# Layernorm roots taken for two tiles at once, and a new instruction order: a two-layer attention and MLP kernel

## The chip, the cores and the metric

One core of a Trainium2 chip. The metric is the device time of one execution in microseconds (us); most executions of one kernel agree within 0.3%. TensorE does the matmuls, VectorE (DVE in the profile) and ScalarE (ACT) the elementwise work, GpSimd (POOL) a little of it, and SyncE (SP) issues transfers.

## The reference

Two layers over x of 2048 rows and 512 columns, 32 heads of 16. Each has a linear attention with softmax features and a gated MLP, both behind a layernorm:

```python
def _A_ref(x, wqkv, w_phi, wo):
    q, k, v = ...                                  # x @ wqkv, 32 heads of 16
    pq, pk = q @ w_phi, k @ w_phi                  # per head
    phi_q = concat([softmax(pq), softmax(-pq)]); phi_k = the same of pk
    kv, z = phi_k^T v, sum(phi_k)                  # sums over all 2048 rows
    return (phi_q @ kv / (phi_q @ z + 1e-6)) @ wo
def _B_ref(x, W_gate, W_up, W_down):
    return (relu(x @ W_gate) * (x @ W_up)) @ W_down
for layer in range(2):                             # same weights twice
    x = x + _A_ref(layernorm(x), ...); x = x + _B_ref(layernorm(x), ...)
```

The sum over all rows in `kv` matters here: no attention of a layer can start before the keys of all 16 tiles of 128 rows are done. So a layer has a key stage, a seam, and then attention and MLP tiles; keys of layer 1 run beside the MLP of layer 0.

## The kernel before

The kernel describes each piece of work as an `op` with an engine, a planned cost in ns and a priority (`DUE`), and lets a small planner simulate the engines and write the program in the planned order. `DUE` (2117 numbers) and `PLACE` (301 bits, which of two engines takes an eviction or a scaling) were found by a search over planned time. The normalisation in front of the keys is this:

```python
ACT1 = (190, 297)                    # planned ns: how long the engine is taken, when the result is there
ACT0 = (95, 205)
SUMS = (8 * 40, 8 * 40 + 170)        # the eight key-sum matmuls of a tile ("kvz")
...
def norm_A(l, t, due, after, how):
    _, mv, rs, ln = st[l, "A"]
    a = stats(l, "A", t, due, after)                      # VectorE: bn_stats, bn_aggr
    a = op("ACT", ACT1, due, lambda: nc.scalar.activation(
        out=ln[:, t:t + 1], in_=mv[:, t, 1:2], func=AF.Ln, scale=1.0, bias=eps[:]), [a, c_eps], name="ln")
    a = op("ACT", ACT0, due, lambda: nc.scalar.activation(
        out=rs[:, t:t + 1], in_=ln[:, t:t + 1], func=AF.Exp, scale=-0.5), [a], name="rstd")
    xn = Buf(p_xn)
    n = op("DVE", SCALE, due, lambda: nc.vector.tensor_scalar(...), [a], [xn], name="xnA", port=True)
    ...                                                   # then turned by a transfer or by TensorE
```

1 / sqrt(variance + eps) is exp(-0.5 ln(variance + eps)), on one column per tile: 128 rows, one number each. The planner itself, cut:

```python
def plan(ops):
    ...
    for e, cand in open_.items():       # of every engine: what could start first; DUE decides among equals
        ...
        o = min((o for t, o in at if t <= first + 1), key=rank)
    ...
    clock[o.eng] = t + occ              # engines run their instructions strictly in this order
```

The softmax here doesn't subtract the row's maximum and nothing guards it: scores larger than these inputs give would overflow.

Of the kernel before, what the change touches and what calls it, by code (L numbers as in the profile page):

```python
# [8 lines left out]
P = 128  # L9
D = 512  # L10
H = 32
# [196 lines left out]
SUMS = (8 * 40, 8 * 40 + 170)  # L208
# [12 lines left out]
class K:  # L221
# [9 lines left out]
    "0000010100000000000000000000000001000000000001000000010000010000111000100010000011100010000000001100"  # L231
    "1110100001101000000001001111110001111111000111101111011101100100001001010011001101100101101011001010"
    "0111100111000000000111000001000000011010011000110100110100010010010010011111011011010111101111110001"
    "1"
)
PHI = dict(POOL=("POOL", "POOL"), DVE=("DVE", "DVE"), BOTH=("DVE", "POOL"))
PHI0 = ["POOL", "POOL", "DVE"] * 5 + ["BOTH"]
BLOCKS = ((1, 1, 2, 4, 4, 2, 2), (1, 1, 2, 4, 4, 2, 1, 1))
# [4 lines left out]
    171312045, 171176422, 171176382, 171108352, 171198950, 171077496, 171191852, 171044825, 171078679, 171078698,  # L243
    171075562, 172890511, 176979114, 171233483, 169157194, 169158347, 169158293, 172028606, 169159557, 172030067,
    175144900, 173911508, 175144538, 171845769, 169157815, 171893840, 172460034, 171325700, 171787868, 171042634,
    171000808, 171921057, 170984535, 171039910, 171020854, 171061543, 170544187, 171018809, 171804656, 171138113,
    171042055, 171921054, 166325450, 171843476, 171894266, 172913174, 172651099, 171841824, 172662070, 171803244,
    170856605, 171671995, 171013294, 171049523, 171011469, 170882211, 170861860, 170773832, 171088096, 171173941,
    166032751, 171021263, 171024027, 165980719, 171010636, 170972794, 170819202, 170901748, 170120315, 170882262,
    171029170, 171058781, 171028664, 170882214, 170773339, 170644736, 171176421, 170834144, 170500271, 171024600,  # L250
    171023816, 171671545, 170881567, 170973450, 170924320, 170862256, 171733328, 171027555, 171028689, 170104438,
    170987569, 171023551, 171017586, 170995073, 171010979, 171010010, 167097015, 171025767, 171021114, 170976230,
    171009963, 170940900, 170707416, 170903149, 170861679, 170895382, 170987736, 170805774, 171134539, 171029304,
    171015238, 170840189, 171086712, 170868324, 172856244, 171023850, 170972541, 170882265, 170862137, 170938874,
    171078382, 171074459, 171076295, 170781572, 171024964, 171027552, 170806858, 171027495, 171045955, 171031024,
    170994249, 171063885, 171044941, 170994211, 171021566, 171025728, 170861672, 170773342, 171004053, 171050973,
    171041308, 166032748, 171017859, 170995571, 172857251, 170995217, 171021462, 171036003, 171036000, 171021133,
    171034376, 171019328, 171026473, 170901529, 171024967, 170970509, 170994580, 171076245, 171039727, 174124623,
    167096153, 170995703, 170993965, 172856241, 171391510, 169375356, 166303781, 170203837, 171046298, 171045973,
    171020654, 171025772, 171029618, 171031289, 171018943, 171009668, 171040302, 212653769, 170870934, 170529933,  # L260
    171034876, 170993625, 171023605, 170674343, 170471544, 170946591, 173676712, 171046899, 170942347, 170973537,
    170992325, 171016031, 171004733, 170995129, 171046905, 171039117, 171046765, 170882142, 171036586, 171036549,
    170994607, 171035366, 171017772, 171035774, 166304101, 171351583, 171019187, 170346706, 170971352, 171020568,
    171004375, 171003406, 171019334, 170304741, 171357616, 166452149, 166304120, 171079347, 166362383, 171167760,
    171117024, 166253921, 166338723, 171040796, 171047078, 171026685, 169377831, 171021245, 170994356, 170993118,
    36276708, 36035224, 170174038, 170250060, 171018957, 171021288, 171052769, 171039826, 171052600, 171024073,
    170912232, 170912229, 171041278, 171041091, 171026709, 170998266, 170996907, 171023919, 171166970, 170791395,
    170174888, 36033968, 171014267, 166253845, 171052882, 170955784, 170370511, 171069861, 171052009, 171114979,
    171018524, 171021870, 166290380, 169376343, 170080981, 170529851, 171023791, 170744874, 36538735, 169932483,
    167242939, 166340952, 169222540, 171015285, 166253698, 171075807, 171049021, 171048078, 171040769, 171046830,  # L270
    170951770, 171034112, 171019616, 162145965, 166306292, 168062450, 170989765, 170738642, 171014079, 171052180,
    171053152, 171029348, 171107467, 171116988, 171052395, 171052101, 171047241, 171018507, 166291021, 170394652,
    170241606, 169841292, 169839339, 171025410, 36538707, 169011552, 170955744, 171035785, 170982203, 171011859,
    172910993, 171019677, 171107459, 171053563, 171019442, 170965939, 171116604, 170396198, 170371650, 170946958,
    170908940, 171025481, 169342071, 170739641, 170936868, 171053246, 171052141, 170955698, 171107296, 170969038,
    171023612, 171023814, 171022273, 170966052, 166242691, 170739300, 170739634, 172357143, 171546744, 169010552,
    36035209, 171416052, 171078698, 171044839, 171075311, 170998783, 171032340, 170924317, 170900084, 170081843,
    171086886, 170990356, 171026585, 173042630, 173042922, 173042517, 168321289, 172879342, 173042568, 168321051,
    172927323, 170992379, 172910634, 171038768, 170968444, 171030324, 171014479, 173212841, 171391944, 166303271,
    170994206, 171041364, 171020312, 171051951, 171058190, 170965859, 171041907, 169841329, 171055174, 171052230,  # L280
    170942705, 170942434, 171085553, 171076047, 171053056, 171145237, 171076497, 171074528, 171014605, 171056526,
    171051703, 171087793, 171055202, 171055199, 173107373, 171046402, 171075427, 171142525, 171076401, 171076133,
    171040387, 171077324, 171053025, 173106718, 171076475, 171076472, 171151969, 171055262, 171076461, 165027616,
    171071476, 171071476, 171021261, 171071470, 166364733, 170933205, 171071456, 171072557, 166583114, 166634328,
    170763740, 171064949, 171064956, 167452684, 171029994, 171034997, 171028062, 174965392, 171024521, 171067273,
    171075410, 171025877, 171066819, 171039121, 171025885, 171074446, 171043144, 171024040, 178726974, 174950080,
    178814041, 171074432, 170065497, 171030810, 167260056, 171030866, 170939768, 171027739, 172713143, 170846670,
    171027934, 171030090, 171029521, 171029163, 171042670, 170921361, 172866657, 170417020, 170585755, 170756076,
    169426177, 167510585, 170739334, 171054335, 170496052, 171026814, 171033593, 171037765, 171030610, 170922766,
    170611363, 171028464, 171030272, 168112842, 166271274, 166270840, 166270101, 169191803, 170915073, 171067239,  # L290
    169457441, 171028842, 168543918, 171030184, 170611592, 171035872, 171030051, 170924132, 170923368, 171030620,
    170915873, 170906849, 171068641, 170774900, 174317953, 170772708, 172787245, 174802385, 171548595, 177175587,
    170194011, 171030804, 171031467, 171031553, 171031404, 169172838, 169173200, 171030929, 171031335, 171031355,
    168543946, 162962369, 162963842, 170874511, 171383560, 170476373, 171046401, 171033853, 170289040, 171030586,
    168965534, 170924236, 171030926, 171037386, 171031635, 171030844, 170775025, 170870650, 170774436, 170503270,
    170503425, 168543850, 170673934, 170673801, 171546738, 171032639, 170471129, 171030697, 171031009, 171031310,
    171031944, 170801875, 171025213, 171031797, 171025213, 171024587, 170509377, 170340672, 170301702, 170301316,
# [161 lines left out]
def kernel(  # L459
# [194 lines left out]
    def norm_A(l, t, due, after, how):  # L654
# [9 lines left out]
            op1=Alu.mult), [a], [xn], name="xnA", port=True)  # L664
        c, i = t // C, t % C
        return turn(xn, lambda: xnTA[c][:, :, i * P:(i + 1) * P], how, due, n, [], [], "xnTA",
                    XPOSE if l else XPOSE_LOADS)


    class Keys:  # L670
# [346 lines left out]
```

## Time and profile before

| | before |
|---|---|
| time, us | 387.9 median of 6 (387.68 to 388.77) |
| span of the profiled run, us | 386.3 |
| busy, us: TensorE / VectorE / ScalarE / GpSimd | 374.1 / 315.3 / 212.0 / 45.3 |
| matmul and weight-load records | 2787 and 2831 |

Busy TensorE is recorded with overlapping matmuls, and 44 matmul records are missing from this trace, so it can't be compared between kernels. I use **TensorE's lost time** instead: I go through the weight loads, whose records are complete, give each the spacing that its matmul has where matmuls run back to back (0.216 us for 512 columns down to 0.0325 for 65), and note when each sum of work is reached. The time that passes less the work that is done is what TensorE lost. All of the program's work is about 367 us.

### The profile page before, as it was taken

How to read it: one execution, taken by the hardware profiler on the slowest of the kernel's cores; microseconds unless marked ns; L12 is line 12 of the kernel's file. 1: busy time of each engine (PE TensorE's matmuls, PEld its weight loads, DVE VectorE, ACT ScalarE, POOL GpSimd, SP SyncE). 2: the span in 40 equal slices, each digit the busy share in tenths (PEclk: the TensorE clock that was granted, in tenths of full speed). 3: DMA queues.
4: the chain of work that ended last, by engine and by line, in shares of the span. 5: the costliest groups of instructions: out<-in, count | busy, mean ns of one | idle time of the engine just before them, and what ended most of it. 6: DMA issues, size and time to landing. Idle time of an engine off the chain costs nothing.

```text
span 386.3 us, 7626 instructions
## 1 busy us (share of the span) xinstructions
PE 374.1 (97%) x2787; PEld 225.2 (58%) x2831; DVE 315.3 (82%) x799; ACT 212.0 (55%) x559; POOL 45.3 (12%) x46
## 2 busy tenths in 40 slices
PE   8989998999999999999999999999999999999996
PEld 4544454877654445445766755587865445447585
DVE  7999999999999889838875776899998999544244
ACT  5989988654456314554555669975435411422131
POOL 0433810000021000202222224000000000000000
PEclk9999999999999999999999999999999999999999
DMA  8469740232323224301101100013322234001020
GB/s 228 124 159 240 173 120 1 33 60 56 75 35 63 30 41 65 60 15 26 24 14 22 27 3 1 2 31 61 76 62 63 30 69 97 14 14 49 14 63 29
DMA packets 60869, 22.83 MB, mean 59 GB/s; under 512 B 52672, under 2 KB 59808, under 8 KB 60832
## 3 DMA queue, kind: packets, MB, share of 16 engines
q1 hardware_dynamic: 60416, 21.95, 26.2%
q8 instruction: 22, 0.36, 0.4%
q10 hardware_dynamic: 416, 0.39, 0.3%
q14 instruction: 15, 0.12, 0.1%
HBM read 7.91 MB, written 2.10 MB: 26 GB/s over the span
## 4 chain that ended last, share of the span: by engine, by line
PE 76%; DVE 9%; ACT 3%; issue 2%; DMA 2%; POOL 0%; DVEq 0%; ACTq 0%
PE b L874 34%; PE b L907 19%; PE b L810 6%; PE b L682 4%; PE b L688 4%; PE q L778 3%; PE b L850 2%; ACT Eq L764 2%; PE b L760 2%; DVE sk L693 2%; PE q L719 1%; DVE phiK L702 1%; DMA oT<-o 1%; DVE bstA L651 1%; DMA xnTA<-xn 1%
## 5 line engine op out<-in xcount | busy, mean ns | idle before, releaser
L874 PE MATMUL b<-xnTB,wgu 128*128 128x128 bf16 (+2 forms) x1192 | 150.1, 279 | 0.7 <-ACT xnTB L604 0.3
L874 PEld LDWEIGHTS <-wgu 128*128 128x128 bf16 x1200 | 97.3, 98 | 42.7 <-issue 0.4
L878 ACT ACTIVATE gu<-b 128x512 bf16<-128x512 f32 (+1 forms) x83 | 48.1, 584 | 67.0 <-PE b L874 63.0
L907 PE MATMUL b<-wd,hT 128*128 128x512 bf16 (+2 forms) x348 | 81.8, 372 | 0.8
L702 POOL TENSOR_TENSOR phiK<-ek,sk 128x512 bf16<-128x512 bf16 x40 | 44.6, 1133 | 191.3 <-ACT sk L698 106.1
L907 PEld LDWEIGHTS <-hT 128*128 128x128 bf16 (+1 forms) x363 | 34.5, 98 | 35.0 <-DVE hT L882 0.3
L882 DVE TENSOR_TENSOR hT<-gu 128x512 bf16<-128x512 bf16 (+1 forms) x83 | 33.5, 408 | 16.5 <-ACT gu L604 14.9
L685 ACT ACTIVATE ek<-b 128x512 bf16<-128x512 f32 x64 | 36.6, 626 | 14.1 <-PE b L682 14.0
L693 DVE TENSOR_REDUCE sk<-ek 128x64 f32<-128x1024 bf16 x32 | 38.6, 1208 | 6.8 <-ACT ek L685 5.8
L605 DVE CAST gu<-b 128x512 bf16<-128x512 f32 (+1 forms) x42 | 28.0, 669 | 15.7 <-PE b L874 15.7
L764 ACT ACTIVATE Eq<-b 128x512 bf16<-128x512 f32 x64 | 36.1, 631 | 1.7 <-PE b L760 0.9
L604 ACT CAST gu<-b 128x512 bf16<-128x512 f32 (+1 forms) x41 | 23.2, 565 | 22.8 <-PE b L874 21.8
L682 PE MATMUL b<-Wk,xnTA 128*128 128x512 bf16 x122 | 32.1, 379 | 1.6 <-DMA xnTA<-xn 1.2
L810 PE MATMUL b<-wo,oT 128*128 128x512 bf16 x125 | 32.4, 379 | 0.7 <-DMA oT<-o 0.4
L688 PE MATMUL b<-wv,xnTA 128*128 128x512 bf16 x120 | 31.9, 379 | 1.0 <-ACT xnTA L604 0.3
L760 PE MATMUL b<-xnTA,Wq 128*128 128x512 bf16 x125 | 30.9, 379 | 0.2
L914 DVE SCALAR_TENSOR_TENSOR X<-b,rsB,X 128x512 bf16<-128x512 f32 (+1 forms) x33 | 23.8, 730 | 7.5 <-PE b L907 7.2
L778 PE MATMUL q<-R,Eq 128*128 128x144 bf16 x256 | 27.8, 226 | 1.4 <-ACT DS L604 0.8
L604 ACT CAST N<-q 128x384 bf16<-128x384 f32 (+1 forms) x60 | 26.7, 466 | 4.1 <-DVE pr L803 2.9
L778 PEld LDWEIGHTS <-Eq 128*128 128x128 bf16 x256 | 20.3, 98 | 11.8 <-issue 2.2
L814 DVE TENSOR_TENSOR X<-X,b 128x512 bf16<-128x512 bf16 x32 | 21.4, 675 | 5.0 <-PE b L810 4.7
L855 ACT ACTIVATE gr<-b 128x192 bf16<-128x192 f32 (+1 forms) x19 | 5.8, 308 | 31.8 <-PE b L850 31.8
(70 smaller groups left out, 408.9 us busy)
## 6 DMA issues: line engine op xcount, KB each, us to landing
out_dram<-X SPq DMA_DIRECT2D x15, 128.0 KB, 1.8
X<-in_A_x_dram SPq DMA_DIRECT2D x6, 256.0 KB, 3.4
wgu<-in_B_W_gate_dram SPq DMA_DIRECT2D x4, 344.0 KB, 3.7
wgu<-in_B_W_up_dram SPq DMA_DIRECT2D x4, 344.0 KB, 3.6
wd<-in_B_W_down_dram SPq DMA_DIRECT2D x5, 256.0 KB, 4.9
wv<-in_A_wqkv_dram SPq DMA_DIRECT2D x2, 256.0 KB, 4.3
wo<-in_A_wo_dram SPq DMA_DIRECT2D x4, 128.0 KB, 3.4
oT<-o SPq DMA_TRANSPOSE x28, 2.4
```

The costliest lines, as they stand in the source:

```text
L604: both = {"ACT": ("ACT", act(cols), lambda: nc.scalar.copy(out=out_(), in_=in_()), False), "DVE": ("DVE", dve(cols), lambda: nc.vector.ten ...
L682: k = op("PE", mm(4, 512), due, lambda: [nc.tensor.matmul(kp.t[:], lhsT=xnTA[c][:, b, cols], rhs=Wk2[:, b, :], start=(b == 0), stop=(b == ...
L688: v = op("PE", mm(4, 512), due_v, lambda: [nc.tensor.matmul(vp.t[:], lhsT=xnTA[c][:, b, cols], rhs=wv[:, b, :], start=(b == 0), stop=(b == ...
L693: a = op("DVE", SUM16, due, lambda: nc.vector.tensor_reduce(out=sk.t[:], in_=ek.t[:].rearrange("p g s (h f) -> p (g s h) f", f=DH), axis=A ...
L702: e.tensor_tensor(out=ph.t[:].rearrange("p g s (h f) -> p (g s h) f", f=DH)[:, lo:lo + n], in0=ek.t[:].rearrange("p g s (h f) -> p (g s h) ...
L760: q = op("PE", mm(4, 512), due(c, b), lambda b=b, qp=qp: [nc.tensor.matmul(qp.t[:], lhsT=Wq2[:, m, b * P:(b + 1) * P], rhs=xnTA[c][:, m, : ...
L764: done.append(op("ACT", act(512), due(c, b), lambda b=b, s=s, qp=qp: nc.scalar.activation(out=Eq[c][:, b, s, :], in_=qp.t[:], func=AF.Exp, ...
L778: pe.append(op("PE", mm(len(groups), GE), due, lambda ps=ps, groups=groups: [nc.tensor.matmul(ps.t[:, n * GE:(n + 1) * GE], lhsT=Eq[c][:, ...
L810: a = op("PE", mm(4, 512), due + 3, lambda: [nc.tensor.matmul(yp.t[:], lhsT=oT.t[:, b, :], rhs=wo[:, b, :], start=(b == 0), stop=(b == NB ...
L874: nc.tensor.matmul(ps.t[:, q * W:(q + 1) * W], lhsT=wgu[:, s, b, g * P:(g + 1) * P], rhs=xT.t[:, b, 0:W], start=(b == 0), stop=(b == NB - 1))
L878: nc.scalar.activation(out=gu.t[:, 0, 0:cols], in_=gp.t[:, 0:cols], func=AF.Relu)
L907: nc.tensor.matmul(yp.t[:, 0:c1 - c0], lhsT=h.t[:m, f * W + i * P:f * W + (i + 1) * P], rhs=wd[:m, f, c0:c1], start=(f == 0), stop=(f == N ...
```

## The change

Its intent: fewer of the small ScalarE instructions in the first stage, where ScalarE is full; a truer planned cost of the key sums; and an order found by a new search that also varies when the engines start. The core of the diff (the tables of 2117 and 2105 priorities and the placement bits are cut):

```diff
-SUMS = (8 * 40, 8 * 40 + 170)
+RLN, REXP = ((150, 265), (203, 318)), ((145, 262), (198, 315))
+SUMS = (8 * 32.5, 8 * 32.5 + 170)
 PLACE = (  ... 109 of 301 bits differ ...
+PAIRN, PAIRK = 4, T
 DUE = (    ... every number differs ...
-    def norm_A(l, t, due, after, how):
+    def norm_A(l, tiles, dues, afters, hows):
-        a = stats(l, "A", t, due, after)
+        t0, n = tiles[0], len(tiles)
+        seen = [stats(l, "A", t, due, after) for t, due, after in zip(tiles, dues, afters)]
-            out=ln[:, t:t + 1], in_=mv[:, t, 1:2], ...
+            out=ln[:, t0:t0 + n], in_=mv[:, t0:t0 + n, 1], ...
-            out=rs[:, t:t + 1], in_=ln[:, t:t + 1], ...
+            out=rs[:, t0:t0 + n], in_=ln[:, t0:t0 + n], ...
+        for t, due, how in zip(tiles, dues, hows):       # then each tile is scaled and turned as before
...
     for t in range(T):
-        xT.append(norm_A(0, t, ...
+        if len(xT) <= t:
+            ts = [t] if t < PAIRN else [t, t + 1]
+            xT += norm_A(0, ts, ...
```

The key roots (`lnk`, `rk`) can now be paired too, but `PAIRK = T` leaves them single.

## The prediction

> **What bounds the kernel now.** I read four views in this order: the tenths of the page, for where engines are full; a table of long stretches, for how much; the chain of waits at the seams; and the groups by line, for what one instruction costs. First the tenths and then the table by stage of the kernel before (columns: length of the stretch, then busy us and instructions of each engine, clock, DMA share, GB/s).
>
> ```profile
> span 386.3 us, 7626 instructions
> PE 374.1 (97%) x2787; PEld 225.2 (58%) x2831; DVE 315.3 (82%) x799; ACT 212.0 (55%) x559; POOL 45.3 (12%) x46
> PE   8989998999999999999999999999999999999996
> DVE  7999999999999889838875776899998999544244
> ACT  5989988654456314554555669975435411422131
> ```
>
> ```profile
> 0.00:57.00 57.00, 52.97 (x377) 27.57 (x385) 53.27 (x103) 50.01 (x145) 21.45 (x25) 1.00 0.70 177
> 57.00:70.00 13.00, 10.91 (x105) 7.00 (x104) 12.12 (x43) 11.41 (x34) 0.00 (x0) 1.00 0.01 2
> 70.00:232.00 162.00, 160.94 (x1147) 96.59 (x1162) 136.41 (x337) 82.99 (x217) 19.87 (x18) 1.00 0.22 39
> 232.00:250.00 18.00, 17.27 (x127) 9.28 (x128) 13.20 (x38) 17.69 (x46) 3.95 (x4) 1.00 0.01 1
> ```
>
> The reader is to see two kinds of stage. From 70 to 232 us, and again after 250, TensorE is full and nothing else is: what happens on ScalarE or VectorE there is free as long as data come in time. In the first 70 us VectorE and ScalarE are full as well (cut into tens of us, both are at 9.0 to 10.0 of 10 from 10 to 50 us), and in 57:70 TensorE has the largest hole. Around 240 us ScalarE alone is full: 17.69 of 18.00.
>
> How much is there to win at all? TensorE's work follows from the matmul counts and the spacing that the chain shows where matmuls run back to back: four of 512 columns in 0.86 us (0.216 each), eight of 256 in 0.87 (0.109), 112 of 128 in 6.25 (0.056), eight of 192 in 0.66 (0.082), three of 144 in 0.19 (0.0625), 24 of 65 in 0.78 (0.0325). Counting matmuls by their weight loads, since 44 matmul records are missing: K, V, Q and output projection 512 x 0.216 = 110.6; gate and up 320 x 0.216 + 400 x 0.109 + 480 x 0.056 = 139.6; down 341 x 0.216 + 22 x 0.109 = 76.1; tail of gate and up 128 x 0.082 = 10.5; attention 256 x 0.0625 = 16.0; key sums 256 x 0.0325 = 8.3; turns and folds about 6.6. The sum is 367.7 us of 386.3. The 18.6 us left hold about 1.2 us before the first matmul, about 3.2 after the last, and about 4 of waiting in the first 10 us for loads and the warm-up. **Some 10 us of idle TensorE remain**, nearly all of it between 10 and 70 us and around 245 and 305 us. Faster by over 2% means 7.8 us: almost all of those holes. That alone caps the prediction.
>
> The first of those holes is between keys and MLP of layer 0. The chain there (start us, length us, what) is:
>
> ```profile
> 50.95 1.21 DVE sk L693
> 52.16 3.02 DVE phiK L702 x5
> ...
> 56.22 1.89 PE b L760 x8
> ...
> 63.76 0.70 DVE pr L803
> ...
> 66.40 0.81 PE b L810 x3
> ...
> 68.28 2.84 PE b L874 x48
> ```
>
> The last keys' sums and scalings on VectorE end the key stage, then queries, the first attention tile (small VectorE work), the projection, and only at 68.28 does the MLP begin to feed TensorE. The counterpart in layer 1 is one line of the same view, 15 exponentials of the queries in a row on ScalarE:
>
> ```profile
> 235.53 7.28 ACT Eq L764 x15
> ```
>
> **What the Trainium skill says.** "ScalarE: Activation LUTs", section "What ACT_TABLE_LOAD costs" (its last paragraph): an ACTIVATE with a pointer bias takes about 280 ns + 0.833 ns per column, one with immediates 186 + 0.833, and neighbours overlap by about 93 ns. So the price of these one-column roots is fixed cost, and a second column is nearly free. The trace agrees at its floor: the logarithm has a minimum of 278 ns and a median of 295, the exponential 186 and 203; the means are longer because the queue is crowded:
>
> ```profile
>   L657 ACT ACTIVATE lnA<-mvA,eps x32: 278/295/465, 4.3 to 227.9; 128x1 f32<-128x1 f32 x32
> L659 ACT ACTIVATE rsA<-lnA x32: 186/203/387, 4.7 to 228.2; 128x1 f32<-128x1 f32 x32
> ```
>
> "Perfetto Trace Analysis", section "Identifying the Most-Contended Engine", says that matmul busy time is a bad measure of TensorE's headroom because matmuls are pipelined. The trace agrees: one 512-column matmul is recorded with 379 ns and issues every 216, so the 97% hides holes; hence the sum above.
>
> **The change part by part.** (1) Roots in pairs. Tiles 4 to 15 of layer 0 lose 6 logarithms and 6 exponentials. Net of the overlap of 93 ns these are worth about 278 - 93 = 185 and 186 - 93 = 93 ns of ScalarE each, so 6 x 0.28 = **1.7 us** of ScalarE in the first 40 us. (Busy means of 346 and 261 ns in that stage would give 3.6, but overlapped time is counted twice there.) The column added costs 0.8 ns. The price: the even tile's normalisation now waits for the odd tile's statistics, 0.68 + 0.17 us of VectorE. With four buffers for normalised tiles and the transfers that turn them taking microseconds, this is slack unless TensorE starves for keys; it did wait for a turned tile only 1.2 us in one place.
>
> (2) Key roots stay single: the new code could pair them, but the pairing starts at tile 16 of 16. No gain or loss there. The buffer for key sums grows, which costs nothing.
>
> (3) The cost that the planner takes for a key-sum matmul falls from 40 to 32.5 ns. The trace says 0.78 us for 24, so the new value is true: the planner was late by 8 x 7.5 = 60 ns per tile, 1.9 us over 32 tiles. That moves no instruction by itself; it makes the planned order meet the real one better.
>
> (4) The new order and placement. I paired the 0/1 string of both versions with the movable instructions in their order of creation; the count for before matches the trace (24 scalings on VectorE, 40 on GpSimd). 109 of 301 placements change. In the keys of layer 0 VectorE gives two scalings to GpSimd (2 x 0.73 = 1.5 us) and takes one V eviction (0.68) and one folded weight (0.69): **net 0.1 us less**. ScalarE loses that V eviction (0.66) and weight (0.61): **1.3 us less**. In layer 1 the scalings on VectorE go from 11 to 17 and attention evictions on VectorE from 18 to 13; those fall mostly in 70 to 250 us, beside a full TensorE.
>
> Sum for the first stage: ScalarE 3.0 us lighter, VectorE as before, GpSimd 2.3 us heavier with room (21.45 of 57). VectorE is the fuller engine, at 10.0 of 10 from 20 to 40 us, so **ScalarE's 3.0 us do not come off the end of the key stage**. They let some five more query exponentials (0.63 us each) run before 57 us. Ten of those stand in 57:70, where ScalarE is at 11.41 of 13, and there they delay attention evictions. Three us off one of two co-bound engines, in a stage where either can hold the path, I count as about half: 1.0 to 1.5 us. For the annealing I add nothing certain: perhaps 0.5 us, at either sign up to 2.
>
> **The rivals.** *VectorE remains the bound and nothing moves.* For it: VectorE's 10.00 of 10 and its 0.1 us of relief. Against it: 57:70 is bound by both. Time: 387.5 to 388.5. *The new order closes more holes, with the truer spacing and an order less sensitive to where the engines start.* For it: the holes at 57:70, 245 and 305 us are of order, not of work, some 3.5, 1.3 and 1 us. Against it: the order before was already searched the same way, and TensorE is full elsewhere. Time: 384 to 386. *A new wait takes the place of the removed work*: both tiles of a pair arrive late at the keys, or the extra scalings on GpSimd, 1.13 us against 0.73 on VectorE, finish late, or the order fits its planner better than the chip. For it: the turned tile is the one thing TensorE waited for in the key stage. Against it: one wait of 1.2 us only. Time: 389 to 391. *Loads* (DMA share 1.00 from 30 to 40 us) would hide the gain if the weights of the MLP came late; they were landed before 57 us, and no wait for them shows.
>
> **Range and chances.** 388.05 less 1.2 (ScalarE at half) less 0.3 (order) is 386.5. Two us either way for the luck of an order, a bit more on the slow side, gives 384.4 to 389.2. Faster by over 2% needs 380.3 or less: 0.02. Slower by over 2% needs 395.8, which only a badly misplanned order gives: 0.02.
>
> **What would show it.** Right: 26 instead of 32 roots of each kind, ScalarE busy some 3 us less before 57 us, VectorE the same there, the first gate matmuls of the chain starting about 1 us before 68.28, and the distance from there to the end unchanged. Wrong: the first gate matmul at the same time (VectorE held), or later with waits for turned tiles in front of key matmuls, or a gain that arises after 70 us (then it was the order alone).

## More of the kernel before

All runs told here were classed as fast. Within that class there are still two kinds: most have a mean granted TensorE clock of 0.999 or 1.000, some one of 0.994 to 0.996. I call the second kind **runs with a clock dip**; the first experiment shows what is in them.

## The result, and the profile after

| | before | after |
|---|---|---|
| time, us (median of 6) | 387.9 (387.68 to 388.77) | 390.0 (389.58 to 390.76) |
| span of the profiled run, us | 386.3 | 387.8 |

The ratio is 1.0052, 95% interval 1.0039 to 1.0066. Ratios here are the mean time of one kernel's fast runs over that of the other's of the same rounds, so they are not quite the ratio of the medians quoted. So the changed kernel is half a per cent **slower**, clearly, and outside my range; by the 2% rule it counts as the same. A second run of it gave 1.0057. Three of the changed kernel's six runs have a clock dip and take 390.4 us on the mean, the other three 389.8; so some 0.3 of the 2.1 us goes with dips.

The page's head and the table by stage of the changed kernel, to be held against those in the prediction (code lines moved: L874 is now L893, L907 is L926, L764 is L783):

```profile
span 387.8 us, 7667 instructions
PE 376.6 (97%) x2832; PEld 224.4 (58%) x2832; DVE 310.7 (80%) x784; ACT 217.2 (56%) x566; POOL 39.0 (10%) x42
```

```profile
0.00:57.00 57.00, 53.38 (x388) 26.97 (x389) 52.30 (x103) 49.77 (x132) 23.41 (x27) 1.00 0.68 177
57.00:70.00 13.00, 10.55 (x104) 6.87 (x103) 11.95 (x42) 10.97 (x34) 0.00 (x0) 1.00 0.00 1
70.00:232.00 162.00, 161.10 (x1160) 96.02 (x1158) 135.55 (x337) 83.57 (x220) 15.27 (x15) 1.00 0.21 39
232.00:250.00 18.00, 17.43 (x128) 9.29 (x126) 14.73 (x35) 17.63 (x46) 0.34 (x1) 1.00 0.01 2
```

ScalarE has 13 instructions fewer before 57 us (132 for 145), and is recorded busy for as long as before (49.77 for 50.01 us). The two kernels look alike: the loss can't be read from busy shares. The roots did change as meant, by form (columns: shapes and count, busy us, mean ns, idle before):

```profile
L660 ACT ACTIVATE lnA<-mvA,eps 128x1 f32<-128x1 f32 x20 | 5.3, 293 | 11.7 <-DVE mvA L653 11.5
L662 ACT ACTIVATE rsA<-lnA 128x1 f32<-128x1 f32 x20 | 3.9, 202 | 0.2
L660 ACT ACTIVATE lnA<-mvA,eps 128x2 f32<-128x2 f32 x6 | 1.8, 317 | 0.7 <-DVE mvA L653 0.7
L662 ACT ACTIVATE rsA<-lnA 128x2 f32<-128x2 f32 x6 | 1.3, 216 | 0.0
```

The means of the two forms differ by 24 and 14 ns, but they come from different stages. From the start of a two-column root to the start of the next instruction it is 186 to 202 ns for the logarithm (where ScalarE doesn't idle) and 93 or 94 for the exponential, against a median of 185 and 93 for one column in the kernel before: the second column is free within some 10 ns.

TensorE's lost time says where the two microseconds came from. The columns are stretches of work done, in us; stretch 60 to 366 begins at about 74 us of the clock in both. Single profiled runs, all three without a clock dip, so a difference of 0.3 means nothing by itself.

| work done, us | 10-60 | 60-130 | 130-140 | 140-230 | 230-240 | 240-270 | 270-275 | 275-366 | 60-366 |
|---|---|---|---|---|---|---|---|---|---|
| before | 7.0 | -0.1 | 0.1 | 0.7 | 0.9 | 0.1 | -0.1 | 0.6 | **2.2** |
| after | 6.5 | 0.8 | 0.5 | -0.1 | 1.9 | 0.0 | 0.6 | 0.0 | **3.7** |
| after, second run | 6.4 | 1.0 | 0.4 | -0.1 | 1.9 | 0.0 | 0.3 | 0.1 | **3.6** |

At 60 us of work the changed kernel is 0.4 us ahead (73.8 us on the clock for 74.2), which is hardly more than its own two traces differ (0.3 us). All of the loss comes later, 1.5 us of it in these traces, in four places: around 80, 152, 250 and 288 us. The largest is the seam of layer 1. The chain of waits there, first before and then after (start us, length us, what):

```profile
248.28 0.62 DVE bstB L651
...
249.13 0.35 DVE xn L829
...
249.56 0.38 PE b L642 x4
249.94 0.86 PE b L810 x4
...
250.99 0.33 PE b L850 x4
251.32 1.34 PE b L874 x24
```

```profile
249.46 0.55 DVE N L606
250.01 0.60 DVE bstB L652
...
250.89 0.35 DVE xn L848
251.24 0.52 DVE X L833
...
251.80 0.70 DVE xnTB L606
...
252.55 0.50 PE b L869 x4
253.05 1.79 PE b L893 x32
```

At 251 us both kernels have done 235 us of work. In the old one the first MLP tile of layer 1 is normalised at 249.13, its turned copy is evicted by ScalarE, and gate matmuls run at 251.32. In the new one an eviction of attention (N) stands on VectorE ahead of the statistics, a residual addition (X) ahead of the eviction of the turned tile, and that eviction itself was placed on VectorE: gate matmuls run at 253.05. The two smaller holes are turning transfers that land late, in front of a key matmul and of the tail of gate and up:

```profile
148.33 4.26 DMA xnTA<-xn
...
152.63 1.04 PE b L691 x4
```

```profile
286.83 2.42 DMA xnTB<-xn
...
289.30 0.83 PE b L869 x8
```

### The profile page after: what moved, and what is told of

Read it like the earlier page. It is cut to its first block, busy times and chain, and to the rows that moved or that the text cites. A ratio compares the mean times of both kernels' runs of the same rounds, so it can differ in the third digit from the quotient of the medians.

```text
span 387.8 us, 7667 instructions
## 1 busy us (share of the span) xinstructions
PE 376.6 (97%) x2832; PEld 224.4 (58%) x2832; DVE 310.7 (80%) x784; ACT 217.2 (56%) x566; POOL 39.0 (10%) x42
## 4 chain that ended last, share of the span: by engine, by line
PE 78%; DVE 11%; ACT 4%; DMA 4%; issue 2%; SPq 0%; DVEq 0%; ACTq 0%
PE b L893 34%; PE b L926 18%; PE b L829 6%; PE b L779 4%; PE b L697 4%; PE b L691 4%; PE b L869 3%; PE q L797 3%; DVE bstA L652 2%; DVE sk L702 2%; DMA xnTA<-xn 2%; PE q L738 2%; ACT Eq L783 1%; DVE xn L667 1%; DMA oT<-o 1%
## 5 line engine op out<-in xcount | busy, mean ns | idle before, releaser
L893 PE MATMUL b<-xnTB,wgu 128*128 128x128 bf16 (+2 forms) x1200 | 151.1, 279 | 0.0
L893 PEld LDWEIGHTS <-wgu 128*128 128x128 bf16 x1200 | 97.8, 98 | 43.7
L926 PE MATMUL b<-wd,hT 128*128 128x512 bf16 (+2 forms) x363 | 83.8, 373 | 0.0
L721 POOL TENSOR_TENSOR phiK<-ek,sk 128x512 bf16<-128x512 bf16 x36 | 38.3, 1083 | 192.7 <-ACT sk L712 137.7
L926 PEld LDWEIGHTS <-hT 128*128 128x128 bf16 (+1 forms) x363 | 34.5, 98 | 34.1 <-DVE hT L901 0.9
L605 ACT CAST gu<-b 128x512 bf16<-128x512 f32 (+1 forms) x49 | 27.8, 568 | 18.8 <-PE b L893 18.8
L783 ACT ACTIVATE Eq<-b 128x512 bf16<-128x512 f32 x64 | 36.2, 625 | 1.7 <-PE b L779 1.6
L605 ACT CAST N<-q 128x384 bf16<-128x384 f32 (+1 forms) x66 | 29.4, 465 | 5.8 <-DVE pr L822 3.5
L606 DVE CAST gu<-b 128x512 bf16<-128x512 f32 (+1 forms) x34 | 23.0, 675 | 9.8 <-PE b L893 9.6
L652 DVE BATCH_NORM_STATS2 bstA<-X 128x6 f32<-128x512 bf16 x32 | 21.0, 679 | 1.4 <-DMA X<-in_A_x_dram 1.3
L822 DVE TENSOR_TENSOR pr<-N,w 128x1024 bf16<-128x1024 bf16 x32 | 21.7, 682 | 0.4
```

What stands on the lines that cost most here:

```text
L605: both = {"ACT": ("ACT", act(cols), lambda: nc.scalar.copy(out=out_(), in_=in_()), False), "DVE": ("DVE", dve(cols), lambda: nc.vector.ten ...
L721: e.tensor_tensor(out=ph.t[:].rearrange("p g s (h f) -> p (g s h) f", f=DH)[:, lo:lo + n], in0=ek.t[:].rearrange("p g s (h f) -> p (g s h) ...
L783: done.append(op("ACT", act(512), due(c, b), lambda b=b, s=s, qp=qp: nc.scalar.activation(out=Eq[c][:, b, s, :], in_=qp.t[:], func=AF.Exp, ...
L893: nc.tensor.matmul(ps.t[:, q * W:(q + 1) * W], lhsT=wgu[:, s, b, g * P:(g + 1) * P], rhs=xT.t[:, b, 0:W], start=(b == 0), stop=(b == NB - 1))
L926: nc.tensor.matmul(yp.t[:, 0:c1 - c0], lhsT=h.t[:m, f * W + i * P:f * W + (i + 1) * P], rhs=wd[:m, f, c0:c1], start=(f == 0), stop=(f == N ...
```

## The experiments

The planner is chaotic: one changed number moves everything behind it. To undo one part alone I therefore took the choice of order away from the planner. The helper `forced` walks a given list `SEQ` with the planner's own clocks and buffers, and `FLIP` lists the operations that change engines:

```diff
-    return plan(ops)
+    return forced(ops)       # SEQ: the numbers of the operations in the order wanted
```

**Theory A**: the loss comes from the new order of the later stages. **Theory B**: it comes from the pairs and the new first stage. Theory C came up later: planned costs that are too short on VectorE.

### 1. The new start alone (new_start) and the new rest alone (new_rest)

```diff
+SEQ = changed order up to the planned 61 us, then what is left in the order of before     # new_start
+SEQ = order of before up to the planned 61 us, then what is left in the changed order     # new_rest
```

> The changed kernel's instructions in the changed order up to the planned 61 us (pairs of roots included), then the order and placement of the kernel before. Theory A (the loss comes from the new order of the later stages): the changed trace is level with the old or 0.2 to 0.3 us ahead at 70 us, so the time is 387.5 to 387.9 us, ratio to before 0.999 to 1.000. Theory B (the pairs and the new first stage cost the two us): 389.5 to 390.3 us, ratio 1.004 to 1.006.

> The complement: single roots and the order of before up to the planned 61 us, then the new order and placement. Theory A: 390.0 to 390.4 us, ratio 1.005 to 1.0065, with holes of TensorE near 152, 250 and 288 us. Theory B: 387.7 to 388.3, ratio 1.000.

new_start: 1.0008 (0.9994 to 1.0022). new_rest: 1.0035 (1.0017 to 1.0052), between what the two theories said. All twelve kernels of the experiments gave right results. Lost time of TensorE between 60 and 366 us of work: 2.0 with the old rest (before: 2.2), 3.6 with the new rest (after: 3.7 and 3.6), with 1.9 us of it again between 230 and 240. Theory A holds for most of the loss: it follows the late order, whichever start stands in front of it. new_start is no clean win: it lost 7.8 us up to 60 us of work, for 6.5 in the changed kernel. That isn't the cost of the joint alone, for its profiled run has a clock dip (length of the stretch, busy us and instructions of the engines, clock, DMA share, GB/s):

```profile
63.00:67.00 4.00, 3.67 (x22) 2.08 (x21) 2.74 (x8) 2.28 (x8) 0.00 (x0) 0.57 0.00 0
```

The granted clock is 0.50 for whole microseconds there, some 3.4 us in all, and 1.00 before and after. About 0.5 of the 1.3 us more is lost between 50 and 54 us of work, where the dip is, and 0.5 between 54 and 56, where the kernel before loses as much. Dips have to be kept apart from here on, since they go with the start of the kernel: 21 of 36 runs with the changed start have one, 7 of 54 with the old start, and none of the 18 of the searched orders (experiment 7). Why is not shown. With runs without a dip alone, new_rest is at 1.0031 (four runs), new_start at 1.0009 (two) and the changed kernel's second run at 1.0047 (two): the late order still holds most of the loss.

### 2. The pairs taken apart in the new order (after_single)

```diff
-            out=ln[:, t0:t0 + n], in_=mv[:, t0:t0 + n, 1], ...
+            for u in tiles: out=ln[:, u:u + 1], in_=mv[:, u, 1:2], ...      # and the same for the exponential
```

> The changed kernel, order held, but each pair's logarithm and exponential issued as two one-column instructions again: 12 more instructions, some 1.7 us of ScalarE before 40 us. Theory A with VectorE as the bound of that stage: 390.0 to 390.4, within 0.1% of the changed kernel. If ScalarE's time is on the path, as the prediction counted at half: 390.8 to 391.7.

1.0052 (1.0036 to 1.0068), against 1.0052 and 1.0057 of the changed kernel itself: twelve instructions more cost nothing that five rounds can show. The trace shows 7.0 us lost between 10 and 60 us of work for 6.5 and 6.4, so half a microsecond at most. Five of these six runs have no clock dip and stand at 1.0055, for 1.0047 of the changed kernel's second run without dips: a cost of some 0.3 us is not ruled out.

### 3. The pairs alone in the old order (pairs_only)

```diff
+SEQ = order of before; statistics and roots of tiles 5, 7, ... 15 moved ahead to those of 4, 6, ... 14
```

> The order and placement of before with pairs of roots only: the odd tile's statistics and roots moved ahead to the even tile's, as far as the planner's search of their places found good. If pairing saves time by itself (prediction): 386.8 to 387.5. If it saves nothing on the path (VectorE bound): 387.7 to 388.2. If the earlier statistics and the wait of the even tile cost (Theory B): 388.6 to 390.

0.9989 (0.9973 to 1.0004): between a microsecond faster and 0.2 slower. Up to 60 us of work it is where the kernel before is (74.2 us on the clock in both). Pairing by itself does no harm, so Theory B falls for the pairs, and it brings little, so my expectation of 1.0 to 1.5 us fails. It is not a full test, though: this order puts each pair's exponential directly behind its own logarithm, for which it has to wait, so that a logarithm keeps the next instruction off for 0.33 us and not 0.19. Counted from start to next start, the roots keep ScalarE 0.9 us less than before here, and in the changed kernel 1.5 us less than in after_single (1.7 in its second trace).

### 4. ScalarE loaded instead of relieved (before_double)

```diff
+        again = 2 if l == 0 and t >= 4 else 1
-        a = op("ACT", ACT1, due, lambda: nc.scalar.activation(...), ...
+        a = op("ACT", ACT1, due, lambda: [nc.scalar.activation(...) for _ in range(again)], ...   # the same for ACT0
```

> The kernel before, order held, with the logarithm and the exponential of tiles 4 to 15 issued twice each: 24 more instructions, some 3.4 us of ScalarE before 45 us, twice what pairing takes away and with the other sign. If ScalarE's time in that stage counts at half, as the prediction had it: 1.7 us slower, ratio 1.004. If VectorE is the bound and ScalarE has room: under 0.5 us slower, ratio 1.000 to 1.001. If ScalarE is fully on the path: 3.4 us, 1.009.

1.0122 (1.0105 to 1.0139), which is 4.7 us: more than any of the three expectations. All of it is lost before 60 us of work (78.0 us on the clock for 74.2). I had sized the load wrongly. Here are the same roots on ScalarE's timeline, before and doubled (start us, length us):

```profile
28.64 0.34 ACT L657 ACTIVATE lnA<-mvA,eps 128x1 f32<-128x1 f32 x1
28.82 0.64 ACT L764 ACTIVATE Eq<-b 128x512 bf16<-128x512 f32 x1
29.30 0.26 ACT L659 ACTIVATE rsA<-lnA 128x1 f32<-128x1 f32 x1
29.39 0.64 ACT L604 CAST vext<-b 128x512 bf16<-128x512 f32 x1
```

```profile
29.16 0.65 ACT L658 ACTIVATE lnA<-mvA,eps 128x1 f32<-128x1 f32 x2
29.71 0.58 ACT L766 ACTIVATE Eq<-b 128x512 bf16<-128x512 f32 x1
30.19 0.43 ACT L661 ACTIVATE rsA<-lnA 128x1 f32<-128x1 f32 x2
30.52 0.57 ACT L604 CAST vext<-b 128x512 bf16<-128x512 f32 x1
```

A single logarithm keeps the next instruction off for 0.18 us (28.64 to 28.82), two that write the same column for 0.55. The second doesn't overlap the first. With 0.09 and 0.33 for the exponential that is 12 x (0.37 + 0.24) = 7.3 us of ScalarE, not 3.4 (the medians of all twelve give 6.9), and 4.7 of it reach the end. The bound moved with it. The stretch from 10 to 50 us, before and doubled (columns as above):

```profile
10.00:50.00 40.00, 38.39 (x274) 19.43 (x278) 39.58 (x69) 38.43 (x121) 20.27 (x19) 1.00 0.73 178
10.00:50.00 40.00, 35.67 (x235) 17.20 (x237) 34.96 (x63) 39.23 (x130) 17.64 (x17) 1.00 0.58 160
```

VectorE falls from 39.58 to 34.96 us of busy time, ScalarE is at 39.23, and the chain that ended last runs along ScalarE. That the roots only came later can't be it: no wait of TensorE for a turned tile shows in that trace. So ScalarE's time does count in this stage once there is more of it, and yet taking away some 1.5 us brought next to nothing. Both fit a stage in which two engines are full: loading one makes it the bound, relieving it leaves the other, here VectorE. That relieving VectorE alone would bring something was not tried.

### 5. The holes closed by hand (after_moves, with after_again as the control; pairs_moves)

```diff
 # after_moves: SEQ of the changed kernel, with
+K group of 152 us behind the gate group that follows it; a gate group ahead of the projection of 80 us
+transfer oT ahead of the third of three xnTB transfers: behind it (288 us)
+two evictions of attention behind the normalisation of 250 us; eviction of the turned tile to ScalarE
 # pairs_moves: SEQ of pairs_only, with three moves of the same kind at 156, 248 and 304 us
```

> The changed kernel unaltered, as the control of this call: ratio to before 1.004 to 1.0065, with the holes of TensorE near 80, 152, 250 to 253 and 288 us as in its first trace.

> The changed kernel with instructions moved at the four holes only: one K group behind the gate group that follows it (152 us), a gate group ahead of a projection (80 us), one turning transfer of attention behind one of the MLP (288 us), and at 250 us two evictions behind the first MLP tile's statistics and the eviction of its turned tile on ScalarE. Theory A (the loss is these holes): 1.2 to 1.8 us less than the control, ratio to before 1.000 to 1.002. If the holes are only where the lateness of something else shows: within 0.3 us of the control, other holes in their place.

> The order of before with pairs of roots, and the same kind of repair at its own three holes after 70 us: a V group behind an up group (156 us), a turn behind an attention group (248 us), a gate group ahead of a projection (304 us). If holes can be closed by moving the waiting group back: 0.6 to 0.9 us under before, ratio 0.9975 to 0.9985; if not, as before, 0.999 to 1.000.

after_again: 1.0057 (1.0044 to 1.0069). after_moves: 1.0073 (1.0058 to 1.0088). pairs_moves: 1.0014 (1.0002 to 1.0026). Moving by hand failed, with or without dips: four of six runs have one in both, and the others take 390.1 us on the mean for 389.9 of the control. Only one of the four moves surely did what it was for: the loss between 130 and 140 us of work is gone. The hole at 288 us has 0.3 us for 0.6 in the first trace, but the control, without the move, has 0.3 too. The hole at 80 us came back at 83, and the one at 250 us grew from 1.9 to 2.7 us of loss. Its chain shows why:

```profile
250.40 0.55 DVE N L779
250.95 0.12 DVE DS L779
...
252.41 0.39 ACT N L778
...
252.85 0.35 PE q L970 x3
253.20 0.33 PE b L1042 x4
```

The evictions that I moved back hold the two attention banks, and the attention matmuls (L970) stand ahead of the MLP's in TensorE's order; so they waited, and the MLP behind them. In pairs_moves a new hole of 0.5 us opened at 318 us. A hole in such an order is where lateness shows, not a thing that can be moved away by itself.

### 6. The old order from layer 1's seam on (new_until_207)

```diff
+SEQ = changed order up to the planned 207 us, then what is left in the order of before
```

> The changed kernel in its own order up to the planned 207 us, then the order and placement of before. Theory A says that the passage to layer 1's MLP (240 to 255 us, 1.9 us of idle TensorE in the changed order against 0.9 before) and the hole at 288 us hold over half of the loss: 388.9 to 389.4 us if before is 388.2, ratio 1.0015 to 1.003, with about 0.9 us lost between 240 and 255 us. If the loss lies before 207 us or moves: 1.005 and more.

1.0038 (1.0016 to 1.006): the interval holds both what I expected and no gain, so by time alone it is undecided. Five of its six runs have a clock dip, which may be what pushes it up: the one without takes 389.09 us, 1.002 of the kernel before and inside my range, but it is one run. The trace has 1.2 us lost between 230 and 240 us of work (changed 1.9, before 0.9) and 2.6 between 60 and 366 (3.7 and 2.2), but the run lost 8.7 us before 60, where its order is the changed kernel's, which lost 6.5: its clock is at 0.50 for 3.4 us from 63.6 us on. The seam answers to the order there, though not cleanly.

### 7. Orders searched anew (search_tight, search_slack, search_slack_pairs)

The traces say that the planner's costs are slightly off: start to start, instructions of VectorE take some 12 ns longer than planned (a product of 1024 columns 602 ns for 589) and ScalarE's evictions 12 ns less (478 for 491). With the measured costs I searched further from the old order, once for the shortest plan, and once for the shortest mean of three plans, of which one has slower transfers and one a slower VectorE.

```diff
+SEQ, FLIP = from a search of 25 minutes; plan costs of VectorE and ScalarE as measured
```

> The kernel before, its order searched further by me with instruction costs measured in the traces (VectorE some 12 ns longer an instruction, ScalarE 12 ns shorter than the planner has them) for the shortest plan alone. Theory C (costs that are too short on VectorE are what the chip adds): 1 to 1.5 us under before, ratio 0.996 to 0.9975. If a tight plan does not hold on the chip: level or slower, 0.999 to 1.005.

> As search_tight, but the shortest mean of three plans: measured costs, turning transfers a quarter slower, VectorE 2% slower. If slack in the order is what the chip pays for: 1.5 to 2.5 us under before, ratio 0.9935 to 0.996, and better than search_tight. If not: no better than search_tight.

> As search_slack, with the roots of tiles 4 to 15 in pairs, from the order of pairs_only. If pairing is worth something once the order is made for it: 0.3 to 1 us under search_slack. If it is worth nothing: within 0.3 us of it.

search_tight: 1.0108 (1.0084 to 1.0133). search_slack: 1.0014 (0.9992 to 1.0036). search_slack_pairs: 1.0005 (0.9985 to 1.0024). The gain that I expected came in none of them. The tightest plan is the slowest kernel of the three by almost 1%, with 9.3 us lost up to 60 us of work and 4.6 after. Theory C falls in its simple form: truer costs don't make a plan true. Slack seems to matter, as far as one search of each kind can show it: the two orders that were asked to stand some lateness lose 2.2 and 1.9 us after 60 us of work, as little as the kernel before, and differ by nothing that their intervals show, pairs or not. No order of mine beats the kernel before; search_slack_pairs and pairs_only equal it.

## Why the prediction was wrong

The prediction said 386.5 us, 384.4 to 389.2; it was 390.0. The "within 2%" and its cap (at most some 10 us of idle TensorE to win) were right. By its own steps:

- **The bound.** Right. TensorE's work is the same in both kernels, and time is decided by its holes, in the first 70 us and at the seam of layer 1.
- **Roots in pairs.** Right as a count: 26 of each kind, and as a size: from start to next start the roots keep ScalarE 1.5 to 1.7 us less (the changed kernel's two traces against after_single), for 1.7 predicted. The wait of the even tile for its partner did no harm (pairs_only).
- **"Three us off one of two co-bound engines ... I count as about half: 1.0 to 1.5 us."** The first step that failed. Measured, the pairs alone are worth 0.4 us (0.9989, not clear of zero), nothing in the new order, and the changed kernel as a whole is 0.4 us ahead at 60 us of work. ScalarE was not busy 3 us less before 57 us but 0.2, and 25 query exponentials ran before 57 us for 24 before, not five more. The first rival, that VectorE remains the bound, fits this stage, and the mirror experiment (before_double) shows why half is no fair share: ScalarE's load counts, its relief hardly does.
- **"For the annealing I add nothing certain: perhaps 0.5 us."** (The sum then took 0.3.) The step that decided the sign. The new order loses 1.5 us more than the old after 60 us of work, and this goes with the late order wherever it is put (new_rest against new_start). I had taken 70 to 232 us as free, since TensorE alone was full there; but a new order can open holes in a full stage, and it did at 80 and 152 us.
- **The truer spacing.** I held that it makes the planned order meet the real one better. It also took 60 ns per tile of planned TensorE time away, which had been slack for the other engines. That this is what made the new order fragile is argued, not shown; timed by the planner's own clock, both at the new spacing, the new order is 382.8 us long and the old one 382.1, so the search had not found a shorter plan, only one for other costs. That could have been asked before any run, and it has the sign right.
- **The rivals.** The third, "the order fits its planner better than the chip", 389 to 391 us, is what came, though with the waits at the seam of layer 1 and at late transfers and not in front of the first keys. I gave it too little room: my range ended at 389.2.
- **The signs to look for.** The first gate matmuls start at 68.41 us, for 68.28 before: "the same time (VectorE held)", as written under wrong. From there to the end it is 1.4 us longer (387.8 - 68.41 against 386.3 - 68.28).

What stays open: which single lateness starts the loss at 250 us, since moving the instructions that stood in the way didn't close it, and why the old order is as good on the chip as it is. The profiled runs hold 1.5 of the 2.1 us between the medians; the two profiled runs have no clock dip, about 0.3 of the rest goes with the dips of other runs, and what is left is spread. Why the changed start has more dips is open too.

## What to carry to other kernels

In a stage where two engines are full, measure relief and load apart: that an added microsecond costs says nothing about a removed one. A new search of an instruction order is a change of its own with its own sign; separate it from the code change by running the change in the old order, and put its range, here half a per cent, on both sides. Where the bound engine runs through without gaps, judge an order by the bound engine's lost time stretch by stretch, look at the granted clock of each stretch before blaming the order for a loss, and don't trust the shortest plan: of the orders searched here it was the slowest on the chip. Time old and new order with one set of costs before running them.

## What the Trainium skill lacked or had wrong

- "TensorE: Matmul & The Clock Gate", section "Back-to-back issue gap", gives 81 ns for 128 columns and 131 ns for 512 as the sustained gap of a stream of weight loads and matmuls, and says that its formula for a single matmul, 216 ns at 512, over-counts there. This case agrees with the formula and not with the sustained figures: four matmuls of 512 columns, each with its own weight load, take 0.86 us, and 112 of 128 columns 6.25 us (56 ns each).
- "ScalarE: Activation LUTs", section "What ACT_TABLE_LOAD costs", has neighbouring ACTIVATEs overlap by 93 ns, which the roots here do; it doesn't say that two that write the same column don't overlap. Here two logarithms of 0.29 to 0.34 us took 0.65 together and kept the next instruction off for 0.55 us, one alone for 0.18. In after_single, where the two write neighbouring columns, the second starts 0.185 to 0.20 us after the first; in before_double, where they write the same column, 0.31 to 0.36.
- "Perfetto Trace Analysis", section "Identifying the Most-Contended Engine", warns of matmul busy time but not of missing records: one trace here has 2787 matmuls for 2831 weight loads, another of the same work 2832 for 2832. Weight loads counted with their spacing gave a measure that repeats within some 0.3 us between two traces of the changed kernel, both without a clock dip.
